# Exponentials of running sums written without a step from a stepped PSUM read, one decay transfer in place of two, and a new program order

## Chip, cores, metric

One core of a Trainium2 chip. The time is the device time of one execution in microseconds, median of several. The record calls a run slow when it lies over 1.5% above the fastest of its kernel.

PE is the matmul engine, ACT the scalar engine (logarithms, exponentials, cosines), DVE the vector engine, POOL the general engine GpSimd, and SP issues most transfers; "ACTq" and "SPq" are the queues of an engine, which issue its transfers. In lines of a timeline the first number is the start in us, the second the duration, and brackets hold the idle time of the engine just before and what ended it. A step in an access means that the elements taken one after another do not lie side by side.

## The reference, cut

A gated linear attention (4 batches, 8 heads, 768 steps, head size 48) and a feed-forward block with `h * cos(h)`:

```python
for t in range(S):
    state = alpha[:, :, t, :, None] * state + np.einsum('bhd,bhe->bhde', k[:, :, t], v[:, :, t])
    y[:, :, t] = np.einsum('bhd,bhde->bhe', q[:, :, t], state)
...
h = x @ w_in              # x: 3072 x 384, w_in: 384 x 2048
g = h * np.cos(h)
return (g @ w_out).astype(np.float32)
```

## The kernel before

The sequence is cut into 24 chunks of 128 steps. For two chunks at a time (a "block" below) ACT takes the logarithm of alpha, PE forms the running sums by a triangular matrix, and ACT takes two exponentials of them: with the sign turned (`icp`, for k) and as it is (`cp`, for q). The last row of `cp` is the decay over a chunk. Two transfers spread it over the partitions, for the state's update.

```python
cum_new = ps.tile([C, 2, 512], FP, tag="big", bufs=3)      # PSUM, shared with scores and feed-forward
...
cp_new = cpool.tile([C, 2 * D, 2, NP], FP, tag="cpl")       # s, (parity d), chunk, head pair
icp_new = cpool.tile([C, 2, HD], FP, tag="icpl")
...
nc.scalar.activation(out=icp_t[g][:, lo : lo + n], in_=cum_ps[g][:, lo : lo + n, 0:HD],
                     func=AF.Exp, scale=-1.0)
nc.scalar.activation(
    out=cp_t[g][:, :, lo : lo + n].rearrange("s x i p -> s i p x"),
    in_=cum_ps[g][:, lo : lo + n, 0:HD].rearrange("s i (p x) -> s i p x", p=NP),
    func=AF.Exp, scale=1.0)
for a in range(2):
    nc.scalar.dma_start(
        out=tot[64 * a : 64 * a + D, g % 4, lo : lo + n],
        in_=cp_t[g][C - 1 : C, a * D : (a + 1) * D, lo : lo + n])
```

The feed-forward block takes the same kind of PSUM buffer and gives it back only after ACT's cosine and DVE's product:

```python
t = ps.tile([C, HF, C], FP, tag="big", bufs=3)              # ff1: PE, 24 matmuls
nc.scalar.activation(out=c_sb, in_=h_ps[j, half], func=AF.Sin, bias=halfpi, scale=1.0)   # act
nc.vector.tensor_tensor(out=g_new, in0=h_ps.pop((j, half)), in1=c_t.pop((j, half)), op=ALU.mult)  # gate
```

The program order is a string of units (`T` transposes, `A` scores, `F`/`G` feed-forward halves, `f_`/`g_` their cosines, `w9` nine warm-up products and so on), given as one fixed text; each engine runs its share of it in that order.

Of the kernel before, what the change touches and what calls it, by code (L numbers as in the profile page):

```python
# [9 lines left out]
FP = mybir.dt.float32  # L10
BF = mybir.dt.bfloat16
AF = mybir.ActivationFunctionType
ALU = mybir.AluOpType
# [3 lines left out]
def kernel(  # L17
# [10 lines left out]
    nc = tc.nc  # L28
    B, H, S, D = q.shape
    DM, DF = moe_w_in.shape  # L30
    C = 128
    NC = S // C
    NCH = B * NC
    NP = H // 2
    NF = DF // C
    HF = NF // 2
    HD = H * D
# [6 lines left out]
    consts = ctx.enter_context(tc.tile_pool(name="consts", bufs=1))  # L44
    apool = ctx.enter_context(tc.tile_pool(name="apool", bufs=4))
    inpool = ctx.enter_context(tc.tile_pool(name="inpool", bufs=PF))
    cpool = ctx.enter_context(tc.tile_pool(name="cpool", bufs=4))
# [25 lines left out]
    nc.vector.memset(ub, 0.0)  # L73
    mask_f = consts.tile([C, C], FP, tag="mask_f")
    make_upper_triangular(nc, mask_f, 1.0, diag=True)
    tot = consts.tile([C, 4, 2, NP], FP, tag="tot")
    nc.vector.memset(tot, 0.0)
    m2 = consts.tile([C, 2], FP, tag="m2")
    nc.vector.memset(m2, 0.0)
    nc.vector.memset(m2[0:64, 0:1], 1.0)  # L80
# [3 lines left out]
    w1 = consts.tile([C, 3, DF], BF, tag="w1")  # L84
    w2f = consts.tile([C, NF, DM], FP, tag="w2f")
    w2 = consts.tile([C, NF, DM], BF, tag="w2")

    a_t, q_t, k_t, v_t, cp_t, icp_t = {}, {}, {}, {}, {}, {}
# [44 lines left out]
    def lnset():  # L133
        if table[0] != "ln":
            nc.scalar.preload_act_table_set("natural_log_exp_and_others")  # L135
            table[0] = "ln"
# [9 lines left out]
    cum_ps = {}  # L146
# [12 lines left out]
    def exps(j0, n):  # L159
        lnset()  # L160
        g = j0 // 2
        lo = j0 % 2
        if lo == 0 or n == 2:
            cp_new = cpool.tile([C, 2 * D, 2, NP], FP, tag="cpl")
            icp_new = cpool.tile([C, 2, HD], FP, tag="icpl")
            cp_t[g], icp_t[g] = cp_new, icp_new
        nc.scalar.activation(out=icp_t[g][:, lo : lo + n], in_=cum_ps[g][:, lo : lo + n, 0:HD],  # L167
                             func=AF.Exp, scale=-1.0)
        nc.scalar.activation(  # L169
            out=cp_t[g][:, :, lo : lo + n].rearrange("s x i p -> s i p x"),  # L170
            in_=cum_ps[g][:, lo : lo + n, 0:HD].rearrange("s i (p x) -> s i p x", p=NP),
            func=AF.Exp, scale=1.0)
        for a in range(2):
            nc.scalar.dma_start(  # L174
                out=tot[64 * a : 64 * a + D, g % 4, lo : lo + n],
                in_=cp_t[g][C - 1 : C, a * D : (a + 1) * D, lo : lo + n])

    Em_t = {}

# [3 lines left out]
                                in1=icp.rearrange("s (h d) -> s h d", h=H), op=ALU.mult)  # L183

    def qhat(j):
        cp = cp_t[j // 2][:, :, j % 2]
        eng = nc.vector if j < 2 else nc.gpsimd
        eng.tensor_tensor(out=qhb[:, j % 3, :, 0:D].rearrange("s (p a) d -> s p a d", a=2),  # L188
                          in0=q_t.pop(j).rearrange("s (p a) d -> s p a d", a=2),
                          in1=cp.rearrange("s (a d) p -> s p a d", a=2), op=ALU.mult)  # L190

    def vcast(j):
        nc.gpsimd.tensor_copy(out=vpb[:, j % 3, :, 0:D], in_=v_t.pop(j))  # L193
# [165 lines left out]
    def warmup(n):  # L359
# [12 lines left out]
        "r": lambda h: cast_w1(h, dve, 0, 2), "s": lambda h: cast_w1(h, act_e, 2, 3), "R": cast_w2,  # L372

        "i": lambda j: ln(j, 1), "c": lambda j: cums(j, 1), "d": lambda j: exps(j, 1),
        "l": lambda g: ln(2 * g, 2), "C": lambda g: cums(2 * g, 2), "E": lambda g: exps(2 * g, 2),
        "K": khat, "Q": qhat, "b": vcast, "E_": emask,
        "T": transposes, "t": ev_transposes, "S": state, "u": ev_state,
        "A": scores, "m": mask_scores, "Y": outputs, "y": ev_outputs, "D": x_transposes, "B": ev_x,
# [4 lines left out]
    }  # L383

    ORDER = (
        "v0 a0 a1 i0 w1 c0 d0 q0 b0 Q0 k0 k1 K0 i1 w9 c1 d1 w4 T0 t0 K1 E_0 q1 a2 a3 q2 w4 A0 a4 a5 Q1 S0 u0 "
        "k2 l1 w9 C1 E1 Q2 K2 q3 T1 Q3 v1 b1 k3 K3 l2 w11 C2 E2 q4 t1 a6 m0 Y0 y0 w3 D0 B0 w2 T2 t2 a7 l3 A1 "
        "m1 w4 T3 t3 w4 S1 u1 A2 A3 m2 Y1 C3 E3 k4 v2 Q4 y1 w2 D1 B1 z0 s0 b2 w2 Y2 y2 K4 w3 T4 m3 t4 r0 z1 "
        "w5 D2 B2 A4 r1 z2 s1 w1 S2 E_1 u2 v3 F0 E_2 b3 f_0 F1 f_1 m4 z3 F2 f_2 r2 p0 S3 u3 p1 s2 s3 w3 Y3 v4 "
        "Z1 r3 w2 G0 Z0 y3 p2 g_0 b4 Y4 y4 G1 g_1 D3 Z2 Q_0 Z3 k5 k6 G2 R1 g_2 B3 D4 B4 G3 S4 R0 Q_1 Q_2 V0 "  # L390
        "G4 K5 g_3 R2 R3 q5 F3 Q_3 g_4 W0 e0 u4 F4 f_3 Q5 q6 f_4 K6 V1 Q_4 T5 t5 W1 p3 p4 e1 a8 a9 l4 A5 m5 "
        "Q6 T6 q7 v5 b5 Q7 k7 a10 V2 W2 e2 C4 E4 a11 l5 t6 v6 Y5 y5 V3 K7 T7 W3 t7 D5 B5 A6 m6 A7 v7 C5 b6 S6 "
        "a12 E_3 E_4 u6 e3 V4 Y6 y6 m7 F5 k8 D6 B6 W4 K8 b7 S7 E5 u7 f_5 k9 p5 F6 q8 E_5 f_6 Y7 G5 y7 D7 K9 "
        "q9 g_5 e4 p6 B7 G6 g_6 Q8 T8 t8 F7 f_7 Q9 T9 V5 Q_5 W5 Q_6 t9 p7 A8 m8 A9 k10 a13 v8 b8 v9 b9 K10 S8 "
        "a14 q10 q11 l6 a15 a16 e5 a17 a18 C6 u8 k11 l7 E6 V6 Y8 l8 Q10 Q11 m9 G7 y8 D8 B8 g_7 W6 e6 T10 t10 "
        "F8 f_8 K11 Y9 y9 Q_7 G8 g_8 T11 t11 p8 V7 W7 q12 Q12 q13 q14 D9 Q_8 e7 B9 C7 A10 A11 v10 b10 v11 b11 "
        "v12 v13 E_6 S9 k12 k13 u9 k14 m10 E7 V8 S10 u10 W8 a19 m11 Y10 y10 F9 f_9 a20 a21 Q13 e8 D10 B10 G9 "
        "k15 g_9 K12 T12 p9 K13 Q14 q15 t12 Q_9 F10 f_10 p10 G10 Y11 K14 C8 y11 V9 g_10 E8 b12 Q_10 D11 B11 "
        "W9 S12 A12 K15 l9 l10 b13 T13 A13 u12 F11 S13 m12 u13 G11 k16 e9 k17 k18 Y12 Q15 q16 V10 m13 y12 T14 "
        "D12 f_11 B12 g_11 v14 v15 b14 b15 W10 e10 K16 Y13 G12 T15 p11 y13 A14 v16 Q_11 V11 D13 m14 q17 q18 "  # L400
        "C9 g_12 Q_12 E_7 E_8 Q16 Q17 Y14 y14 W11 A15 m15 S14 E9 F12 u14 G13 K17 f_12 p12 Q18 q19 D14 v17 v18 "
        "T16 F13 g_13 b16 b17 Y15 y15 Q_13 f_13 p13 G14 S15 K18 e11 Q19 V12 u15 T17 k19 E_9 D15 g_14 b18 W12 "
        "e12 A16 A17 Q_14 m16 S16 u16 C10 E10 V13 Y16 m17 y16 G15 v19 b19 S18 u18 g_15 Q_15 F14 f_14 p14 q20 "
        "Q20 Y17 F15 f_15 y17 a22 W13 e13 p15 k20 K19 K20 D16 G16 g_16 Q_16 V14 T18 W14 e14 A18 m18 T19 A19 "
        "m19 F16 V15 f_16 q21 Y18 y18 k21 D17 F17 a23 l11 f_17 Q21 Y19 K21 E_10 p16 y19 p17 G17 W15 e15 T20 "
        "T21 D18 g_17 D19 G18 S19 F18 u19 v20 V16 g_18 f_18 v21 W16 b20 Q_17 Q_18 A20 e16 A21 p18 m20 S20 u20 "
        "m21 V17 C11 E11 b21 Y20 q22 q23 k22 Q22 F19 f_19 W17 y20 k23 Y21 G19 D20 G20 y21 Q23 p19 e17 v22 K22 "
        "S21 b22 g_19 K23 Q_19 V18 W18 g_20 T22 Q_20 e18 F20 V19 f_20 p20 u21 D21 A22 m22 T23 A23 m23 W19 e19 "
        "G21 g_21 Y22 y22 E_11 F21 f_21 S22 v23 u22 V20 Q_21 D22 W20 e20 p21 b23 Y23 y23 G22 F22 g_22 Q_22 "
        "f_22 D23 V21 W21 F23 G23 p22 e21 V22 f_23 p23 g_23 Q_23 W22 e22 V23 W23 e23 "  # L410
    )
    for u in ORDER.split():
        nm = u.rstrip("0123456789")
# [29 lines left out]
```

## Time and profile before

| | before |
|---|---|
| time | 196.99 us, later 197.07 with a fourth run (196.66 to 198.64) |
| profiled execution | 198.02 us, span 196.0 us, a run at the upper edge of these |
| first feed-forward product | 32.15 us |
| last product of the feed-forward | 192.46 us |

Groups by form (line, engine, operation, tiles, sizes, count; busy us and mean ns; idle time before and its releasers), and the decay transfers by tile (ns least/median/most):

```profile
L169 ACT ACTIVATE cp_new<-cum_new 128x768 f32<-128x768 f32 x11 | 17.3, 1569 | 0.0
L167 ACT ACTIVATE icp_new<-cum_new 128x768 f32<-128x768 f32 x11 | 8.9, 809 | 5.3 <-PE cum_new L155 4.3 <-PE t L257 0.5 <-PE t L289 0.5
...
L174 ACTq DMA_DIRECT2D tot<-cp_new x26: 508/588/1232, 7.0 to 161.1; - x26
```

And the timeline of SP's queue near the end (start us, us, what):

```profile
163.86 2.43 SPq L208 DMA_TRANSPOSE t<-kqb  x1
166.38 1.20 SPq L304 DMA_TRANSPOSE x<-t  x1
167.68 1.26 SPq L208 DMA_TRANSPOSE t<-kqb  x1
```

### The profile page before, as it was taken

To read this page: it belongs to the slowest core of one execution; us is meant where nothing else is said; L and a number is where in the kernel's file an instruction comes from. 1 tells how busy PE (TensorE), PEld (TensorE's weight loads), DVE (VectorE), ACT (ScalarE), POOL (GpSimd) and SP (SyncE) were. 2 spreads that over 40 slices of the span, in tenths; PEclk is the share of its full clock that TensorE was granted. 3 is DMA by queue.
4 is the path that set the end of the run, shared out by engine and by line. 5 is a ranking of instruction groups with operands and counts; after the bars stand their busy time and mean duration, and the time that the engine had idled before them with its cause. 6 is when DMAs were issued, how large, how long until landed. Compare 5 with 4: busy or idle time off the path is not lost. (4 is left out here: it accounts for less than half of the span.)

```text
span 196.0 us, 5512 instructions
## 1 busy us (share of the span) xinstructions
PE 180.3 (92%) x2312; PEld 136.2 (70%) x2316; DVE 127.1 (65%) x158; ACT 128.1 (65%) x135; POOL 77.1 (39%) x108
## 2 busy tenths in 40 slices
PE   1996999999998989999999999899899999799993
PEld 0343547798765788795886778769688687587771
DVE  4124669889485578848778595891975954756440
ACT  3446556779566597877787887867668668433450
POOL 4224572402950375480772555767220247022000
PEclk9999999999999999999999999999999999999999
DMA  6999999999997899999269668999893926922012
GB/s 123 204 194 203 218 374 283 373 320 175 216 232 175 178 207 205 216 191 222 65 95 204 148 150 165 176 188 189 184 191 73 239 73 88 189 60 60 20 43 80
DMA packets 124888, 34.24 MB, mean 175 GB/s; under 512 B 118208, under 2 KB 123328, under 8 KB 124864
## 3 DMA queue, kind: packets, MB, share of 16 engines
q1 hardware_dynamic: 119744, 29.14, 72.4%
q10 hardware_dynamic: 5120, 4.76, 7.4%
q8 instruction: 18, 0.29, 0.6%
q14 instruction: 6, 0.05, 0.1%
HBM read 25.17 MB, written 4.72 MB: 152 GB/s over the span
## 5 line engine op out<-in xcount | busy, mean ns | idle before, releaser
L327 PE MATMUL t<-x,w 128*128 128x128 bf16 x1152 | 71.0, 219 | 2.1 <-DVE g_new L341 1.2
L341 DVE TENSOR_TENSOR g_new<-t,c_sb 128x1024 bf16<-128x1024 f32 x48 | 57.6, 1218 | 22.0 <-ACT c_sb L335 20.6
L327 PEld LDWEIGHTS <-w 128*128 128x128 bf16 x1152 | 65.9, 98 | 4.1 <-issue 2.3
L349 PE MATMUL o_new<-w,g_new 128*128 128x384 bf16 x384 | 68.3, 326 | 0.3 <-ACT o_sb L354 0.3
L335 ACT ACTIVATE c_sb<-t,halfpi 128x1024 bf16<-128x1024 f32 x48 | 51.9, 1112 | 15.5 <-PE t L327 12.1
L349 PEld LDWEIGHTS <-g_new 128*128 128x128 bf16 x384 | 36.0, 98 | 21.3 <-issue 0.4
L271 POOL TENSOR_TENSOR ub<-sc,Em 128x384 bf16<-128x384 f32 x16 | 13.3, 829 | 55.1 <-DVE sc L269 51.3
L182 POOL TENSOR_TENSOR kqb<-t,icp_new 128x384 bf16<-128x384 f32 x24 | 23.9, 1001 | 18.2 <-DMA t<-in_k_dram 10.1
L188 POOL TENSOR_TENSOR kqb<-t,cp_new 128x384 bf16<-128x384 f32 x22 | 26.0, 1187 | 12.3 <-DMA t<-in_q_dram 8.0
L241 DVE TENSOR_TENSOR t<-t,mask_f 128x1024 bf16<-128x1024 f32 x24 | 29.0, 1217 | 1.8 <-PE t L232 1.8
L354 ACT ACTIVATE o_sb<-o_new 128x384 f32<-128x384 f32 x24 | 11.7, 487 | 19.0 <-PE o_new L349 19.0
L365 PE MATMUL w_new<-warm 128*128 128x512 bf16 x65 | 19.2, 420 | 1.4 <-DVE warm L57 1.2
L296 DVE CAST t<-t 128x384 bf16<-128x384 f32 x24 | 13.2, 551 | 10.1 <-PE t L289 10.0
L169 ACT ACTIVATE cp_new<-cum_new 128x768 f32<-128x768 f32 (+1 forms) x13 | 19.0, 1460 | 0.0
L142 ACT ACTIVATE lnab<-a_new 128x768 bf16<-128x768 f32 (+1 forms) x13 | 10.2, 792 | 12.8 <-issue 7.0
L335 ACT ACT_TABLE_LOAD x9 | 11.5, 1283 | 7.3 <-DVE t L241 1.7
L221 DVE COPY t<-t 128x1024 bf16<-128x1024 bf16 x13 | 8.9, 687 | 10.1 <-PE t L215 10.1
L365 PEld LDWEIGHTS <-warm 128*128 128x128 bf16 x69 | 6.6, 105 | 11.5 <-issue 6.6
L167 ACT ACTIVATE icp_new<-cum_new 128x768 f32<-128x768 f32 (+1 forms) x13 | 9.9, 760 | 7.0 <-PE cum_new L155 6.0
L193 POOL CAST vpb<-t 128x384 bf16<-128x384 f32 x24 | 12.4, 524 | 3.0 <-DMA t<-in_v_dram 3.0
L135 ACT ACT_TABLE_LOAD x9 | 11.5, 1283 | 2.4 <-ACT o_sb L354 1.6
L269 DVE TENSOR_TENSOR sc<-t,ub 128x384 f32<-128x384 f32 x16 | 8.8, 551 | 4.9 <-PE t L257 4.9
(40 smaller groups left out, 119.4 us busy)
## 6 DMA issues: line engine op xcount, KB each, us to landing
t<-in_v_dram SPq DMA_DIRECT2D x24, 192.0 KB, 4.0
a_new<-in_alpha_dram SPq DMA_DIRECT2D x24, 192.0 KB, 4.0
t<-in_q_dram SPq DMA_DIRECT2D x24, 192.0 KB, 4.1
t<-in_k_dram SPq DMA_DIRECT2D x24, 192.0 KB, 4.0
out_dram<-o_sb ACTq DMA_DIRECT2D x24, 192.0 KB, 3.1
w1f<-in_moe_w_in_dram SPq DMA_DIRECT2D x4, 768.0 KB, 6.8
w2f<-in_moe_w_out_dram SPq DMA_DIRECT2D x4, 768.0 KB, 9.0
tot<-cp_new ACTq DMA_DIRECT2D x22, 1.5 KB, 3.0
```

Of the source, the lines that this page charges most:

```text
L169: nc.scalar.activation(out=cp_t[g][:, :, lo : lo + n].rearrange("s x i p -> s i p x"), in_=cum_ps[g][:, lo : lo + n, 0:HD].rearrange("s i ...
L182: nc.gpsimd.tensor_tensor(out=khb[:, j % 3, :, 0:D], in0=k_t.pop(j), in1=icp.rearrange("s (h d) -> s h d", h=H), op=ALU.mult)
L188: eng.tensor_tensor(out=qhb[:, j % 3, :, 0:D].rearrange("s (p a) d -> s p a d", a=2), in0=q_t.pop(j).rearrange("s (p a) d -> s p a d", a=2 ...
L193: nc.gpsimd.tensor_copy(out=vpb[:, j % 3, :, 0:D], in_=v_t.pop(j))
L241: nc.vector.tensor_tensor(out=t.rearrange("s (h t) -> s h t", h=H), in0=A_ps.pop(j).rearrange("s (h t) -> s h t", h=H), in1=mask_f.unsquee ...
L271: eng.tensor_tensor(out=ub[:, us(j), :, 0:96].rearrange("r p (a e) -> r p a e", a=2), in0=sc.rearrange("r p (a e) -> r p a e", a=2), in1=E ...
L296: nc.vector.tensor_copy(out=t, in_=y_ps.pop(j)[:, 0:HD])
L327: nc.tensor.matmul(t[:, f], w1[:, kk, ft * C : (ft + 1) * C], x_t[j][:, kk], start=(kk == 0), stop=(kk == 2))
L335: nc.scalar.activation(out=c_sb, in_=h_ps[j, half], func=AF.Sin, bias=halfpi, scale=1.0)
L341: nc.vector.tensor_tensor(out=g_new, in0=h_ps.pop((j, half)), in1=c_t.pop((j, half)), op=ALU.mult)
L349: nc.tensor.matmul(o_ps[j][:, 0:DM], g[:, f], w2[:, half * HF + f], start=(f == 0 and half == 0), stop=(f == HF - 1 and half == 1))
L365: nc.tensor.matmul(w_ps, warm[:, 0:C], warm, start=True, stop=True)
```

## The change

Its intent: ACT writes `cp` as it lies in memory and picks the elements out of PSUM with a step instead; each parity's 48 rows are padded to 64, so that one transfer of 128 rows can spread the decay. The padding is cleared once. The program order was made anew.

```diff
+    cpx = consts.tile([C, 4, 2, 64, 2, NP], FP, tag="cpx")
+    nc.vector.memset(cpx[:, :, :, D:64], 0.0)
     tot = consts.tile([C, 4, 2, NP], FP, tag="tot")
-    nc.vector.memset(tot, 0.0)
 ...
-            cp_new = cpool.tile([C, 2 * D, 2, NP], FP, tag="cpl")
             icp_new = cpool.tile([C, 2, HD], FP, tag="icpl")
-            cp_t[g], icp_t[g] = cp_new, icp_new
+            cp_t[g], icp_t[g] = cpx[:, g % 4], icp_new
 ...
         nc.scalar.activation(
-            out=cp_t[g][:, :, lo : lo + n].rearrange("s x i p -> s i p x"),
-            in_=cum_ps[g][:, lo : lo + n, 0:HD].rearrange("s i (p x) -> s i p x", p=NP),
+            out=cp_t[g][:, :, 0:D, lo : lo + n],
+            in_=cum_ps[g][:, lo : lo + n, 0:HD].rearrange("s i (p a d) -> s a d i p", p=NP, a=2),
             func=AF.Exp, scale=1.0)
-        for a in range(2):
-            nc.scalar.dma_start(
-                out=tot[64 * a : 64 * a + D, g % 4, lo : lo + n],
-                in_=cp_t[g][C - 1 : C, a * D : (a + 1) * D, lo : lo + n])
+        nc.scalar.dma_start(out=tot[:, g % 4, lo : lo + n],
+                            in_=cp_t[g][C - 1 : C, :, :, lo : lo + n].rearrange("o a d i p -> o (a d) i p"))
 ...
-        cp = cp_t[j // 2][:, :, j % 2]                            # qhat
+        cp = cp_t[j // 2][:, :, 0:D, j % 2]
 ...                                                               # ORDER, two of its places
-        "v0 a0 a1 i0 w1 c0 d0 q0 b0 Q0 k0 k1 K0 i1 w9 c1 d1 w4 T0 ... C1 E1 ... w11 C2 E2 ...
+        "v0 a0 a1 i0 w1 c0 d0 q0 Q0 k0 k1 b0 i1 w10 c1 d1 K0 w3 T0 ... C1 E1 ... w13 C2 E2 ...
-        ... p20 u21 D21 A22 m22 T23 A23 m23 W19 ...
+        ... p20 u21 A22 m22 T23 A23 m23 D21 W19 ...
```

## The prediction

> **What bounds the kernel now.** I began with the page's busy shares and slices, then cut the span into three stretches, then listed PE's own idle times, then followed each of them back through the timeline. From the page, and from the view of busy time by stretch (columns: stretch, length, busy of PE, weight loads, DVE, ACT, POOL, granted clock, DMA share, GB/s):
>
> ```profile
> PE 180.3 (92%) x2312; PEld 136.2 (70%) x2316; DVE 127.1 (65%) x158; ACT 128.1 (65%) x135; POOL 77.1 (39%) x108
> ...
> 0.00:40.00 40.00, 32.90 (x324) 19.39 (x329) 23.44 (x38) 20.98 (x24) 15.79 (x29) 1.00 0.98 249
> 40.00:180.00 140.00, 134.58 (x1860) 107.43 (x1857) 98.53 (x117) 101.18 (x104) 61.32 (x79) 1.00 0.83 167
> 180.00:196.00 16.00, 12.78 (x138) 9.42 (x135) 5.11 (x5) 5.92 (x7) 0.00 (x0) 1.00 0.16 56
> ```
>
> PE is the bound, at full clock. In the first 40 us a good part of its busy time is filler: 65 warm-up products in the records (19.2 us in the groups). There the true limit is a mixture of arriving loads (DMA share 0.98) and the chain ACT, PE, POOL, DVE that brings up the first chunks. From 40 to 180 us PE is idle only 140.00 - 134.58 = 5.42 us, and the last 16 us are pure matmuls and the store. So nothing that is taken from ACT is worth more than the PE idle time that ACT causes. PE's idle times of 0.2 us or more after 40 us (timeline of PE, in brackets the idle time and its releaser):
>
> ```profile
> 63.50 0.48 PE L155 MATMUL cum_new<-lnab,triu_bf 128*128 128x384 bf16 x2 [0.97 <-ACT lnab L142]
> 72.33 0.34 PE L310 MATMUL t<-ident_bf,t 128*128 128x128 bf16 x3 [0.65 <-DVE t L296]
> ...
> 106.88 1.50 PE L327 MATMUL t<-x,w 128*128 128x128 bf16 x24 [0.35 <-ACT cp_new L169]
> 124.46 0.72 PE L327 MATMUL t<-x,w 128*128 128x128 bf16 x10 [0.72 <-DVE g_new L341]
> 138.24 1.50 PE L327 MATMUL t<-x,w 128*128 128x128 bf16 x24 [0.52 <-DVE g_new L341]
> 164.63 2.76 PE L349 MATMUL o_new<-w,g_new 128*128 128x384 bf16 x16 [0.30 <-ACT o_sb L354]
> 171.63 0.40 PE L232 MATMUL t<-t 48*128 48x128 bf16 x8 [1.26 <-DVE sc L269]
> ```
>
> With one of 0.20 us left out, these make 4.97 us. Behind the first stands this piece of ACT:
>
> ```profile
> 59.02 0.81 ACT L167 ACTIVATE icp_new<-cum_new 128x768 f32<-128x768 f32 x1 [0.47 <-PE t L289]
> 59.73 1.57 ACT L169 ACTIVATE cp_new<-cum_new 128x768 f32<-128x768 f32 x1
> 61.38 1.18 ACTq L174 DMA_DIRECT2D tot<-cp_new  x2
> 62.60 0.84 ACT L142 ACTIVATE lnab<-a_new 128x768 bf16<-128x768 f32 x1 [1.30 <-issue]
> ```
>
> The second exponential runs 1.57 us where the first, same input and same size, runs 0.81; then ACT's queue spends 1.18 us issuing two 1.5 KB transfers, and the engine stands idle for those 1.30 us. The next logarithm is late and PE waits 0.97 us for it. The other waits have the same block upstream, one or two links away. Those at 72.33, 124.46 and 138.24 come behind a gate product on DVE that waited for a cosine on ACT (the DVE timeline shows 1.36, 2.38 and 2.94 us for it), and that cosine stood behind exponentials, the two issues and a table load. The one at 106.88 names the exponential itself: it holds the PSUM buffer. The one at 164.63 follows the block of 158.2 to 163.1.
>
> The one at 171.63 is different. The releaser named is the sum on DVE, but the queue of SP shows another reason: the DMA transpose of chunk 23 was issued only at 167.68, because an x transpose stood ahead of it in the queue. It lands 3.9 us after issue (median of its row), 171.6, which is when PE goes on.
>
> **What the Trainium skill says.** "ScalarE: Activation LUTs", What ACT_TABLE_LOAD costs: an ACTIVATE with immediate scale and bias takes 186 ns + 0.833 ns per element, for any function. The trace agrees for the plain exponential (826 ns by that, 809 measured) and not for the second (1569). "SBUF — State Buffer", Door 1: The DMA port swizzle: SBUF lines have 16 bytes, and each access that moves to a new line pays a penalty. The second exponential writes fp32 with a step of 32 bytes, a new line each time, and its surplus is (1569 - 809)/768 = 0.99 ns an element: agrees in kind. "PSUM — Partial Sum Buffer", Specifications (TRN2): lines of 8 bytes, and it says that patterns that are not contiguous slow matmuls; of ACT reading with a step it says nothing, and no instruction of the trace before does that. This is the open point. "DMA: Bandwidth & Descriptors", Issuing engines are not separate DMA queues: issuing costs sequencer time, "usually small relative to the DMA itself". Here it isn't small: 588 ns median on ACT's queue, against 3.0 us to landing.
>
> **The change, part by part.**
>
> Exponential. The eleven of two chunks now write 384 contiguous elements for each head parity and read PSUM with a step of one head pair. The two of one chunk write runs of four floats, one whole line each. If the read is free, each takes what its plain twin takes: 11 x (1569 - 809) + 2 x (862 - 490) = 8.4 + 0.7 = 9.1 us less ACT, 128.1 to 119.0.
>
> Decay transfer. 26 issues become 13: 13 x 0.588 = 7.6 us less on ACT's queue, 0.6 per block. The one transfer brings 128 rows of 32 bytes instead of twice 48; I keep 3 us to landing. There are also 13 fewer transfers in the rotation of the eight DMA semaphores, for which SP's loads wait (waits of SP name these transfers for 4.9 + 2.2 + 1.3 us).
>
> So each block ends 0.76 + 0.59 = 1.35 us earlier, which is more than any single ACT-caused wait above (0.97).
>
> Setup. The clear of tot (0.09 us) becomes a clear of 1024 floats a row; by the row of 1536 words (1.34 us) an estimated 0.9 us of DVE, done by 4.5 us, before the first product at 6.99. Free. POOL's product keeps its 32-byte step: 1187 ns as before.
>
> Order. The matmuls and their numbers stay. 71 warm-ups instead of 69, 66 against 64 of them ahead of the first feed-forward block: up to 2 x 0.22 = 0.4 us added where they fill no wait. The two last DMA transposes of q and k now stand together ahead of the x transpose, which should remove the 1.26 us at 171.63.
>
> Worth on PE: in the front, the cumulative sum at 19.45 waits 0.98 and the transposes at 15.49 wait 0.47 (for the first decay): at most 1.45, less the 0.4 of warm-ups, about 1.0. In the middle the ACT-made waits are 0.97 + 0.65 + 0.35 + 0.72 + 0.52 + 0.30 = 3.5. At 171.63: 1.26. Ceiling about 5.8 us, 191.2 us.
>
> I don't expect the ceiling. The units are packed so that a PE that comes sooner meets the next thing: DVE is busy 98.5 of the middle 140 us, the DMA engines read about full in much of it (share 1.04 from 120 to 140, 0.91 from 60 to 80), POOL waits 8.0 us for q loads in all. I take a little over half, by judgement: 3.1 us.
>
> **Rivals.** (1) The stepped PSUM read costs what the stepped SBUF write cost. For it: the 8-byte lines; against: the author traded one for the other, and the penalty seen is one of SBUF. I give it one in four. Then a block saves only 0.6 us, half of the middle's waits stay, and the time is about 195.3. (2) The time is set elsewhere, by loads and DVE, and ACT's relief turns into longer idle times of ACT: for it the full DMA slices, against it that PE's middle idle time is nearly all traceable to ACT; about 196. (3) The wider decay transfer lands later and the mask on POOL, which already waits 9.1 us for it in two places, delays the state: adds under 1 us, since those states are needed later. (4) All of it comes back: 191.2.
>
> **Range and chances.** 196.99 - 3.1 = 193.9. Low end near the ceiling, 191.8; high end is rival 2 with some noise, 196.2. The 2% line is 193.05; it needs 3.9 of the 5.8 us, a third or a bit less of my chances. A loss needs new waits of over 3.9 us, which a small reordering hardly makes.
>
> **What would show it.** The second exponential of 128x768 at 0.81 us (right) or near 1.5 (rival 1). ACT busy about 119. 13 decay issues and ACT idle 0.7 us after them, not 1.3. PE idle from 40 to 180 us down from 5.4 to about 3, the wait for the logarithm at 63.5 and the one before the last score products gone. First feed-forward matmul (32.15 now) up to 1 us sooner. If ACT is relieved and PE's idle time is not, the prediction is wrong by rival 2; if PE busy grows, by the fillers.

## The result

189.89 us (189.43 to 190.11, 4 runs) against 197.07 (4 runs): ratio 0.9618, interval 0.9563 to 0.9674. Ratios here are the mean time of one kernel's fast runs over that of the other's of the same rounds, so not quite the ratio of the medians quoted. The time lies below the predicted range (191.8 to 196.2) and even below the "ceiling" of the prediction (191.2).

The page of the changed kernel, its busy time by stretch, the same two groups, and the decay transfers:

```profile
PE 178.9 (95%) x2318; PEld 135.8 (72%) x2318; DVE 127.9 (68%) x158; ACT 119.9 (64%) x135; POOL 77.8 (41%) x108
...
0.00:40.00 40.00, 34.82 (x363) 21.09 (x364) 25.93 (x40) 19.18 (x25) 15.78 (x29) 1.00 0.99 250
40.00:180.00 140.00, 139.69 (x1933) 112.26 (x1931) 100.42 (x118) 99.34 (x108) 62.06 (x79) 1.00 0.84 170
...
L169 ACT ACTIVATE cpx<-cum_new 128x768 f32<-128x768 f32 x11 | 8.9, 805 | 0.0
L167 ACT ACTIVATE icp_new<-cum_new 128x768 f32<-128x768 f32 x11 | 8.9, 809 | 7.9 <-PE cum_new L156 6.6 <-PE t L287 0.8 <-PE t L255 0.5
...
L173 ACTq DMA_DIRECT2D tot<-cpx x13: 477/478/524, 6.6 to 153.3; - x13
```

From 40 to 180 us PE is idle 0.31 us where it was 5.42. Both exponentials take the same. The block that the prediction showed at 59.02 now looks so, and of PE's idle times after 40 us the timeline prints a single one:

```profile
57.67 0.81 ACT L167 ACTIVATE icp_new<-cum_new 128x768 f32<-128x768 f32 x1 [0.79 <-PE t L287]
58.38 0.80 ACT L169 ACTIVATE cpx<-cum_new 128x768 f32<-128x768 f32 x1
59.26 0.49 ACTq L173 DMA_DIRECT2D tot<-cpx  x1
59.79 0.84 ACT L143 ACTIVATE lnab<-a_new 128x768 bf16<-128x768 f32 x1 [0.61 <-POOL vpb L191]
```

```profile
143.57 1.51 PE L325 MATMUL t<-x,w 128*128 128x128 bf16 x24 [0.19 <-DMA x<-t]
```

The logarithm starts 2.1 us after the first exponential, where it was 3.6 us; this is called the length of the block below. SP's queue at the end issues the two transposes of q and k together, and the 16 score products run without a break (SP's timeline, then PE's):

```profile
156.64 3.40 SPq L206 DMA_TRANSPOSE t<-kqb  x2
160.13 1.21 SPq L302 DMA_TRANSPOSE x<-t  x1
...
163.05 0.62 PE L230 MATMUL t<-t 48*128 48x128 bf16 x16
```

Where the 8.1 us between the two profiled spans (196.0 and 187.9) lie: the first feed-forward product comes at 30.49 instead of 32.15 (1.67 us); from there to the last product it takes 153.62 instead of 160.31 us (6.68 us); the end after it is 0.27 us longer. The profiled execution of before was about 1 us above its median, which is why the medians differ by 7.2 us only.

### The profile page after: what moved, and what is told of

Same layout as the page of the kernel before. It is cut to its first block, busy times and chain, and to the rows that moved or that the text cites. A ratio compares the mean times of both kernels' runs of the same rounds, so it can differ in the third digit from the quotient of the medians.

```text
span 187.9 us, 5502 instructions
## 1 busy us (share of the span) xinstructions
PE 178.9 (95%) x2318; PEld 135.8 (72%) x2318; DVE 127.9 (68%) x158; ACT 119.9 (64%) x135; POOL 77.8 (41%) x108
## 4 chain that ended last, share of the span: by engine, by line
PE 86%; DMA 7%; DVE 3%; issue 1%; ACT 1%; SPq 0%; DVEq 0%
PE t L325 32%; PE o_new L347 31%; PE w_new L363 8%; DMA x<-t 5%; PE t L213 3%; PE t L230 3%; PE t L287 2%; PE cum_new L156 2%; PE t L255 2%; DMA a_new<-in_alpha_dram 2%; PE t L284 2%; PE t L308 1%; DVE g_new L339 1%; DVE t L219 1%; DVE t L239 0%
## 5 line engine op out<-in xcount | busy, mean ns | idle before, releaser
L333 ACT ACTIVATE c_sb<-t,halfpi 128x1024 bf16<-128x1024 f32 x48 | 52.6, 1113 | 19.0 <-PE t L325 15.8
L186 POOL TENSOR_TENSOR kqb<-t,cpx 128x384 bf16<-128x384 f32 x22 | 25.9, 1187 | 12.1 <-DMA t<-in_q_dram 8.6
L363 PE MATMUL w_new<-warm 128*128 128x512 bf16 x71 | 20.3, 413 | 1.2 <-DVE warm L57 1.2
L287 PE MATMUL t<-vpb,t 128*128 128x48 bf16 x192 | 11.3, 183 | 0.0
```

The source lines that it names most:

```text
L186: eng.tensor_tensor(out=qhb[:, j % 3, :, 0:D].rearrange("s (p a) d -> s p a d", a=2), in0=q_t.pop(j).rearrange("s (p a) d -> s p a d", a=2 ...
L287: nc.tensor.matmul(t[:, h * D : (h + 1) * D], A_t[j][:, ACOL[h] * C : (ACOL[h] + 1) * C], vpb[:, j % 3, h], start=first, stop=True, skip_g ...
L363: nc.tensor.matmul(w_ps, warm[:, 0:C], warm, start=True, stop=True)
```

## The experiments

The change has three parts, each of which can be done or undone: the exponential (stepped or plain write), the transfers (two or one), the order (old or new). Eight combinations, of which two are the kernels themselves. Theory A, formed on seeing the result: the length of ACT's block is what held PE, and the savings count until PE waits for nothing. Rivals: the order did most of it (B); the code did all (C); the number of transfers counts and not ACT's time (D). All gave correct results, and all medians are of four runs, but for the last two kernels (six and eight). The runs were made beside runs of the kernel before: 197.63, 197.80 and 198.02 us.

| order | write | transfers | median us | ratio to before, interval |
|---|---|---|---|---|
| new | stepped | two | 197.18 | 0.9953 (0.9886 to 1.002) |
| old | stepped | one | 193.01 | 0.9770 (0.9693 to 0.9847) |
| new | stepped | one | 192.22 | 0.9740 (0.9677 to 0.9804) |
| old | plain | two | 192.25 | 0.9696 (0.9621 to 0.9771) |
| new | plain | two | 192.78 | 0.9754 (0.9684 to 0.9824) |
| old | plain | one | 190.40 | 0.9609 (0.9541 to 0.9678) |
| new | plain | one | 189.89 | 0.9618 (0.9563 to 0.9674) |

The medians of the first and the fourth line include one slow run each (199.97 and 194.47); without it they are 197.05 and 191.62. The second, third and fifth line are clearly faster than before, but not clearly by 2% or more.

**1. The order alone.**

```diff
 # kernel before
-    ORDER = (old)
+    ORDER = (new)
```

> The kernel before with the new program order alone (old exponential with the stepped write, two decay transfers). Theory A (the length of ACT's block of exponentials and issues held PE; the order only puts the last two DMA transposes together): 195.5 to 196.5 us, the 1.26 us before the last score products gone, the other PE waits from 40 us on still there. Rival B (the new order is the larger part, because the waits came from the order of the units): 191 to 194 us.

197.18 us (197.05 without the slow run): no difference that the interval shows, and above what theory A had said (195.5 to 196.5). PE's idle times in its profile (its timeline):

```profile
62.95 0.48 PE L155 MATMUL cum_new<-lnab,triu_bf 128*128 128x384 bf16 x2 [1.43 <-ACT lnab L142]
...
124.27 0.94 PE L327 MATMUL t<-x,w 128*128 128x128 bf16 x14 [1.21 <-DVE g_new L341]
...
138.18 1.50 PE L327 MATMUL t<-x,w 128*128 128x128 bf16 x24 [0.95 <-DVE g_new L341]
```

The wait at 171.63 is gone, as the order was to do, but the waits behind ACT's blocks grew: 0.97, 0.72 and 0.52 us in the kernel before, 1.43, 1.21 and 0.95 here. These waits come earlier in the run than the one that is gone, so what they took back is another gain: the first product of the feed-forward came 0.84 us sooner (31.32 us), and at the product of 138.18 us (138.24 before) only 0.06 us of that is left. PE came to the blocks sooner and ACT did not. The wait that is gone did count in this profile: the next feed-forward product starts at 171.76 instead of 173.27 us, and the span is as much shorter (194.5 against 196.0). The medians don't show it: 1.26 us are 0.6%, which lies inside the interval, and the profiled execution is the fastest of the four. Rival B falls.

**2. The code alone.**

```diff
 # changed kernel
-    ORDER = (new)
+    ORDER = (old)
```

> The changed code with the old program order. Theory A: most of the gain stays, 191 to 192.5 us; the wait before the last score products (1.3 us) stays. Rival B (the order is the larger part): 194 to 196 us. Rival C (the code does all of it): 189.5 to 190.5 us.

190.40 us, ratio 0.9609: all of the gain within the intervals, so C rather than A as far as the total goes. Its profile keeps three waits, and the last of them is the one that the order removes:

```profile
131.40 1.51 PE L325 MATMUL t<-x,w 128*128 128x128 bf16 x24 [0.80 <-DVE g_new L339]
143.62 1.51 PE L325 MATMUL t<-x,w 128*128 128x128 bf16 x24 [0.26 <-DMA x<-t]
164.70 0.40 PE L230 MATMUL t<-t 48*128 48x128 bf16 x8 [1.19 <-DMA t<-kqb]
```

Here the releaser is named rightly, the DMA transpose, which supports the reading of the wait at 171.63 in the prediction. On the other side its first feed-forward product comes at 29.78 us, 0.7 us sooner than in the changed kernel. So the order may be worth some tenths, which these rounds do not separate.

**3 and 4. One part of the code at a time, old order.**

```diff
 # changed kernel, old order; run 3: two transfers again, from the padded layout
+        for a in range(2):
+            nc.scalar.dma_start(out=tot[64 * a : 64 * a + D, g % 4, lo : lo + n],
+                                in_=cp_t[g][C - 1 : C, a, 0:D, lo : lo + n])
 # run 4: the stepped write again, into the padded layout, one transfer
+            out=cp_t[g][:, :, 0:D, lo : lo + n].rearrange("s a d i p -> s i p a d"),
+            in_=cum_ps[g][:, lo : lo + n, 0:HD].rearrange("s i (p a d) -> s i p a d", p=NP, a=2),
```

> Old order, the unstepped exponential, still two decay transfers. Theory A: ACT's block is shorter by 0.76 us of the 1.35 us, so a little over half of what the code alone brings: 193 to 194.5 us, ACT busy near 120 us. Rival D (the number of DMA transfers in the rotation of semaphores matters, not ACT's time): 196 to 197 us.

> Old order, the stepped exponential written into the padded layout, one decay transfer. Theory A: the block is shorter by 0.6 us: 194 to 195.5 us, ACT busy near 128 us. Rival D: 191 to 193 us, as far as the code alone goes.

192.25 and 193.01 us. Each part alone brings more than half of what both bring: by the ratios 3.0% and 2.3%, together 3.9%, where the sum would be 5.3%. Each of these is known to 0.7 or 0.8% only; that the savings overlap rests on runs 5 and 6 as well. Both beat what theory A had said of them (193 to 194.5 and 194 to 195.5), since A had shared the gain in proportion. In run 3 ACT is busy 119.2 us, in run 4 128.5. So it is no matter of ACT's busy share, nor of the number of transfers alone (D). In both, the wait for the logarithm shrank: it is 0.20 us in run 3 and 0.28 in run 4, against 0.97. That is about the wait less the saving: 0.97 - 0.76 = 0.21, and 0.97 - 0.6 = 0.37. One saving takes most of this wait, and the second finds only the rest of it to shorten. The other waits shrank less evenly: that behind a gate product at 124.46 from 0.72 to 0.66 and 0.34 us, that for the exponential's PSUM buffer from 0.35 to none in run 3, but it is 0.43 in run 4.

**5 and 6. One part undone, new order.**

```diff
 # changed kernel; run 5: the stepped write as in run 4. run 6: two transfers as in run 3
```

> The changed kernel with the stepped write of the exponential put back (0.76 us of ACT per block of two chunks), one decay transfer, new order. Theory A (PE pays what ACT's block is too long by, so the two savings overlap): 192 to 193.5 us, as the same code had in the old order (193.0). Rival F (new order and new code help one another): 190 to 191 us.

> The changed kernel with the two decay transfers put back (0.6 us of ACT's queue per block), unstepped exponential, new order. Theory A: 191 to 192.5 us, a little under the run before it, as the dose is smaller. Rival F: 190 to 190.5 us.

192.22 and 192.78 us: each part is still worth 1.2 to 1.4% when it is the last one missing, and the order makes no difference to that which the intervals show (rival F falls: old order 193.01 and 192.25). Run 6 lies a little above its expectation. Its profile has the first feed-forward product at 31.41 us, 0.9 us later than in the changed kernel, and waits of PE of 0.20 us for the logarithm and 0.69 us for a DMA transpose.

**7. A useless piece of ACT work behind the exponential.** To see whether ACT's time or the pattern of the write counts:

```diff
 # changed kernel, between the second exponential and the transfer
+        nc.scalar.activation(out=scr[:, lo : lo + n], in_=icp_t[g][:, lo : lo + n], func=AF.Exp, scale=-1.0)
```

> The changed kernel with one more plain ACTIVATE, read by nothing, after each exponential: 768 elements, unstepped, some 0.71 us of ACT per block, and the transfer issued that much later. Theory A: ACT's time alone is what counts, so the same time as with the stepped write put back, 192 to 193.5 us. Rival G (the stepped write harms through its pattern, by the memory and not by ACT's time): 189.5 to 190.5 us.

189.83 us: no cost at all. Taken at face value that kills theory A. ACT's timeline shows that the experiment was built wrongly:

```profile
59.16 0.81 ACT L170 ACTIVATE cpx<-cum_new 128x768 f32<-128x768 f32 x1
59.85 0.84 ACT L174 ACTIVATE scr<-icp_new 128x768 bf16<-128x768 f32 x1
60.04 0.49 ACTq L175 DMA_DIRECT2D tot<-cpx  x1
60.63 0.84 ACT L144 ACTIVATE lnab<-a_new 128x768 bf16<-128x768 f32 x1
```

The filler runs from 59.85 to 60.69, while the queue issues the transfer from 60.04 to 60.53. The engine would have been idle for just that time (0.61 us in the changed kernel), so ACT's busy time rose by 8 us (127.9 against 119.9) and the block is only 0.06 us longer (the table of lengths below). Two runs were made in its place.

**8 and 9. The filler where it cannot hide.**

```diff
 # run 8: ahead of the second exponential
+        nc.scalar.activation(out=scr[...], in_=icp_t[g][...], func=AF.Exp, scale=-1.0)
         nc.scalar.activation(out=cp_t[g][:, :, 0:D, lo : lo + n], ...
 # run 9: behind the transfer
         nc.scalar.dma_start(out=tot[:, g % 4, lo : lo + n], ...
+        nc.scalar.activation(out=scr[...], in_=icp_t[g][...], func=AF.Exp, scale=-1.0)
```

> The changed kernel with the useless ACTIVATE of 768 elements (about 0.71 us) moved ahead of the second exponential, where nothing can hide it: the decays, the release of the PSUM buffer and all that ACT does next come 0.71 us later, as with the stepped write, but nothing is written with a step. Theory A (ACT's time, wherever the pattern): 191.8 to 193 us. Rival G (the pattern of the write itself): 189.5 to 190.5 us.

> The same useless ACTIVATE behind the decay transfer, so that it runs after the issue: only what ACT does next is 0.71 us later, the decays and the PSUM buffer are not. Theory A (the next units of ACT, cosines above all, are what PE waits for): 191.5 to 193 us, close to the run with two transfers put back (192.8). Rival H (the late release of the PSUM buffer is the cost): 189.5 to 190.5 us.

192.16 us (ratio 0.9714, interval 0.9682 to 0.9747) and 191.50 us (0.9678, 0.9642 to 0.9713). Run 8 has the time of the stepped write (192.22) without any stepped write; its ACT timeline shows the filler in the place of the surplus, and PE's timeline has three of the four waits of run 5:

```profile
57.82 0.81 ACT L168 ACTIVATE icp_new<-cum_new 128x768 f32<-128x768 f32 x1 [0.54 <-PE t L289]
58.66 0.84 ACT L170 ACTIVATE scr<-icp_new 128x768 bf16<-128x768 f32 x1
59.41 0.79 ACT L171 ACTIVATE cpx<-cum_new 128x768 f32<-128x768 f32 x1
60.28 0.49 ACTq L175 DMA_DIRECT2D tot<-cpx  x1
...
61.77 0.48 PE L157 MATMUL cum_new<-lnab,triu_bf 128*128 128x384 bf16 x2 [0.46 <-ACT lnab L144]
103.85 1.50 PE L327 MATMUL t<-x,w 128*128 128x128 bf16 x24 [0.47 <-ACT cpx L171]
120.71 1.50 PE L327 MATMUL t<-x,w 128*128 128x128 bf16 x24 [0.44 <-DVE g_new L341]
```

In run 5 these three were 0.65, 0.42 and 0.33 us. So the stepped write cost the kernel through the 0.76 us that it kept ACT, and not through its pattern (G falls). Run 9 delays only what ACT does after the block, since its filler starts when the issue is over:

```profile
59.95 0.84 ACT L176 ACTIVATE scr<-icp_new 128x768 bf16<-128x768 f32 x1 [0.61 <-issue]
```

It costs some 1.5 us against the changed kernel in the same rounds (190.03, run 12), while the wait of 0.47 us for the release of the PSUM buffer does not come up in it (rival H falls as the only cause). The late start of ACT's next units is thus probably the larger part of the cost; the difference of about 0.7 us to run 8 may be the late exponential itself, or the block that is 0.12 us longer there, and lies within what the intervals leave open.

Put together, the times follow the length of ACT's block: from the start of the first exponential to the start of ACT's next instruction other than the second exponential and the filler, median of the eleven blocks of two chunks.

| runs | length of the block, us | time, us |
|---|---|---|
| before; 1 | 3.58; 3.63 | 197 to 198; 197.18 |
| 8 | 3.00 | 192.16 |
| 3, 4, 5, 6, 9 | 2.84, 2.88, 2.89, 2.82, 2.87 | 192.25, 193.01, 192.22, 192.78, 191.50 |
| 7 | 2.18 | 189.83 |
| changed; 2, 10, 11, 12 | 2.12; 2.12, 2.13, 2.15, 2.13 | 189.89; 190.40, 190.04, 189.40, 190.03 |

**10 to 12. Fewer fillers in the front.**

```diff
 # changed kernel; run 10
-    i1 w10 c1 ... l2 w13 C2
+    i1 w9 c1 ... l2 w11 C2
 # run 11
-    i1 w10 c1 ... l1 w9 C1 ... l2 w13 C2
+    i1 w9 c1 ... l1 w4 C1 ... l2 w10 C2
 # run 12: the changed kernel itself
```

> The changed kernel with three warm-up products fewer in the front (9 for 10, 11 for 13), as in the old order. Theory A: the new order's fillers cost the front some 0.6 us, which come back: 189.0 to 189.7 us. Rival: the front is set by loads and DVE, and nothing changes (189.7 to 190.1 us).

> The changed kernel with nine warm-up products fewer in the front (9 for 10, 4 for 9, 10 for 13): if the fillers hold up the front, 188.5 to 189.5 us, first feed-forward product near 29.5 us; if loads and DVE set the front, no change, 189.5 to 190.3 us; if PE's clock falls, more.

> The changed kernel itself, for comparison on this chip: 189.4 to 190.5 us.

190.04 us for run 10, so three fillers are worth nothing that shows; 189.40 for run 11 (ratio 0.9575, 0.9542 to 0.9608), 190.03 for run 12 (0.9594, 0.9568 to 0.9619) in the same rounds. The first feed-forward product comes at 30.25, 29.55 and 30.25 us. Nine fillers fewer bring it 0.7 us forward in the profiles, and 0.6 us in the medians, which the overlapping intervals do not prove. It is no version that one could call better. Run 12 is of use in another way: it is the changed kernel, and its profile has two waits that the first profile does not have (PE's timeline):

```profile
118.72 0.20 PE L284 MATMUL t<-ub,t 128*128 128x96 bf16 x1 [0.60 <-POOL ub L269]
124.84 0.34 PE L230 MATMUL t<-t 48*128 48x128 bf16 x6 [1.14 <-DMA t<-kqb]
```

Its span is 189.4 us against 187.9, and the execution is the second slowest of the eight (191.19 us). The second wait is for a DMA transpose. The first is behind POOL, whose product just ahead (116.69) had waited 1.63 us for a load of q. What is left to wait for differs between executions of one kernel. ACT is not wholly out of it either: runs 2 and 10 have a wait of 0.80 and 0.84 us at a feed-forward product (131.40 in run 2, above) behind a gate product; in run 2 that one waited 2.09 us for a cosine on ACT, which came behind a block and a table load.

## Why the prediction was wrong, by its own steps

- **The exponential** (right): 805 ns, expected 0.81; ACT busy 119.9, expected 119. Rival 1, the costly PSUM read, had one chance in four and did not come.
- **The transfer** (right): 13 issues, 478 ns each where 588 had been taken over; ACT idle 0.61 us behind one, expected 0.7. Rival 3, a later landing, did no harm: the median over all transfers is 3.0 us as before, the eleven of two chunks land after 3.5 us where it was 3.0, but POOL's waits for them fell from 9.1 to 6.1 us.
- **Setup** (right): the clear took 0.91 us, estimated 0.9, and POOL's product 1187 ns as before.
- **The last score products** (right in the profiles): no profile of the new order has this wait; of the four of the old order three have it (0.95 to 1.26 us), and run 3 does not. Where only the order differs (run 1 and before, the changed kernel and run 2), the units behind the wait gain 1.4 us on those ahead of it. The medians don't separate this: the order as a whole, in the four pairs of runs with the same code, gives between 0.5% less and 0.6% more time, each known to about 1% only.
- **The front** (sooner, as predicted; size low): about 1.0 predicted, 1.67 in the two profiles. This is one pair, and run 7, as fast as the changed kernel, has its first feed-forward product at 31.59 us, so how much of it is the change stays open.
- **The ceiling of the middle** (mis-sized): 3.5 + 1.26 = 4.8 us predicted, 6.68 measured. I had added up the idle times that the timeline prints. They begin at the modelled end of a matmul, which stays on record for about 0.22 us although the next one may start after 0.056 us (24 of 128 columns take 1.34 us from the first start to the start of what follows). Counted from start to start, less the median of that for products of the same line and size, the kernel before has twelve waits of 0.15 us or more after 40 us, 7.46 us in all: each of the eight printed ones is 0.16 to 0.19 us longer, and four of 0.24 to 0.30 us did not show among the printed ones. The changed kernel has two of them, 0.63 us. The difference, 6.83 us, is close to the gain of the middle. In run 12's execution of the changed kernel there are three, 2.32 us, and its middle takes 155.28 us, 5.0 less than before.
- **"I take a little over half, by judgement: 3.1 us"** (the step that failed): nearly all came back, in the profile that stands beside the result. I had expected DVE, the loads and POOL to hold PE next. The changed kernel shows DVE at 100.4 of 140 us and a DMA share of 0.84 there, with PE idle 0.31 us: busy shares of that size left room. Of the seven waits of PE that I had traced, six had one cause, ACT's block; counted from start to start these were 0.5 to 1.2 us long, the blocks became 1.35 us shorter by my own sum (1.46 measured), and in this execution nothing else made PE wait for more than 0.35 us. Having traced nearly every wait to one cause, I should have taken all of it, and asked of each other engine for a wait just short of it instead of a high busy share. What I had expected was not empty: in run 12 a load of q and a DMA transpose do hold PE. But even there PE is idle for only 1.81 us from 40 to 180 us, where I had expected about 3 and the first profile has 0.31. Rival 2 rested on those shares alone.
- **The chances** (a third or a bit less for faster by 2%) follow from that step. Rival 4, the ceiling of 191.2, was nearest, and the ceiling itself was 1.3 us too high.

What stays open: how much the new order is worth, which the runs put at less than about one per cent either way, and how the cost of a late block divides between the next units of ACT and the exponential itself.

## What to carry to other kernels

When the waits of the bound engine all trace back to one block on another engine, take the time by which the block gets shorter against each single wait: savings beyond the wait count nothing, and two savings in the same block therefore need not add up (here 3.0% and 2.3% made 3.9%). Measure the waits of a pipelined engine from start to start, not by the idle time that is printed. And when two transposing orders of one copy are to be had, try the step on the PSUM side of ACT with a dense SBUF write (here 805 ns against 1569); then look for what ACT's queue issues in the same place.

## What the Trainium skill lacked or had wrong

- "PSUM — Partial Sum Buffer", Specifications (TRN2), speaks of patterns that are not contiguous for matmuls alone. An ACTIVATE that reads fp32 from PSUM with an innermost step of 384 bytes (one head pair) and writes densely took 805 ns for 128x768, against 809 ns for a dense read: no cost.
- "SBUF — State Buffer", Door 1: The DMA port swizzle, names the penalty of changing 16-byte lines without a figure for ACT's writes: an fp32 write with a step of 32 bytes took 1569 ns instead of 809 for 768 elements, 0.99 ns an element; the writes of four floats in a row, 32 bytes apart, took 484 ns for 384 elements, against 491 dense: no cost.
- "DMA: Bandwidth & Descriptors", Issuing engines are not separate DMA queues, calls the time of issuing usually small. On ACT's queue one issue took 478 to 588 ns (medians of the two kernels), a fifth to a sixth of the 3.0 us to landing, and a second one in 13 places cost 1.4% of the kernel (run 6 against the changed kernel, each by its ratio to before). Where a filler of 0.84 us stood counted: ahead of the issue in the program it ran on beside it and was free (run 7), behind the issue it cost some 1.5 us (run 9).
- "Trainium Kernel Development and Optimization", Performance Expectations, warns that matmul busy time misleads because matmuls are pipelined; the runs agree and add that the idle time does too: 4.97 us printed, 7.46 us from start to start.
